# Sixteen small matmul tiles for the key features of three batches, with new transposes, products and schedule

## The chip, the cores and the metric

The kernel runs on one core of a Trainium2 chip. The metric is the device time of one execution in microseconds (us); smaller is better. Every kernel was run several times, in rounds together with runs of the kernel before on the same chip; experiments 10 to 12 and 13 ran on other chips than 1 to 9, so across them compare ratios and not medians. A run counts as "slow" when it is over 1.5% above the fastest of the same kernel, and "fast" otherwise; on a single core the two words say no more than that. A ratio is the mean time of one kernel's fast runs over that of the other's fast runs of the same rounds, so it is not quite the ratio of the medians quoted beside it.

One more number is used throughout: the **MLP span**, from the start of the first hidden-layer matmul to the start of the last output matmul, both read from TensorE's timeline. Before it lies the head (attention of batch 0), behind it a tail of 3.5 us that is the same in all kernels here.

## The reference, cut to what matters

```python
def phi(x):                                   # r = 8, so 64 features for a row of 32
    a = einsum('rd,bhsd->bhsr', S1, x)
    b = einsum('rd,bhsd->bhsr', S2, x)
    return einsum('bhsi,bhsj->bhsij', a, b).reshape(..., r * r)
q_p, k_p = phi(q), phi(k)                     # q, k, v: 4 batches, 4 heads, 1088 rows, 32 columns
kv  = einsum('bhsf,bhsd->bhfd', k_p, v)
z   = sum(k_p, axis=2)
num = einsum('bhsf,bhfd->bhsd', q_p, kv)
den = einsum('bhsf,bhf->bhs', q_p, z)[..., None] + 1e-06
x = (num / den) transposed to 4352 x 128
h = x @ w_in                                  # 128 x 2048
g = maximum(h, 0) + alpha * minimum(h, 0)
out = g @ w_out                               # 2048 x 128
```

## The kernel before

The program makes its own schedule: each operation is declared with the engines that may do it, an assumed duration in ns, its buffers and a wished time, and a planner orders all of them and gives out the buffers. So the engines execute fixed orders that were tuned for assumed durations. Seven PSUM banks are shared by attention and MLP.

For batches 1 to 3 the old code makes the key features in two halves per batch. VectorE turns 32x32 blocks of k, TensorE multiplies with a block-diagonal S1, S2 (`S12blk`), the result (a and b side by side) is copied from PSUM, and GpSimd forms the 64 products of each row.

```python
def turn(dst, hp=hp):                                     # VectorE, two per half
    nc.vector.transpose(dst...[:, x], k_sb[b][:, 2 * hp:2 * hp + 2]...[:, x])
def fe(e):                                                # TensorE, 16 matmuls per half, 128x32 tiles
    for j in range(n):
        for i in range(0, cnt, aw):
            nc.tensor.matmul(ps(bf)[lo + i:lo + i + aw, j * 64:(j + 1) * 64], sb(bT)[:, ...], S12blk..., start=True, stop=True)
# (copy to ab on ScalarE or VectorE cut)
def pr(e, i=i):                                           # GpSimd: one instruction per half, 16 rows x 64 products
    i0 = bview(at_(a, i * m * r), [[r, m], [1, r], [0, r]])
    i1 = bview(at_(a, r * n * H + i * m * r), [[r, m], [0, r], [1, r]])
    nc.gpsimd.tensor_tensor(out=dst, in0=i0, in1=i1, op=ALU.mult)
res.append(op(en, {"dve": dv(64 * m), "pool": 110 + 64 * m * 1.8}, pr, ...))
```

The products then go into the `kv` matmuls, which sum over all rows and need every product of the batch. The z part is one Gram matmul per group of rows (`zs`), four small ones for the batch's 64 last rows (`zr`), a mask on VectorE (`zm`) and one folding matmul (`finz`):

```python
def zr(e):
    for h in range(H):
        nc.tensor.matmul(ps(bzs)[32 * h:32 * h + r, z0:z0 + r], ab_rest[m][rest, 0, h], ab_rest[m][rest, 1, h], ...)
o = op("pe", 270, lambda e: nc.tensor.matmul(ps(bf)[:, 128:256], E8..., zt(), start=True, stop=True), ..., name=f"finz{b}")
```

Dummy matmuls on constants keep TensorE busy in the head: seven of 512 columns as a warm-up, and a few that the planner puts into idle stretches.

```python
def dummy(n=1):
    for _ in range(n):
        nc.tensor.matmul(PS[:, 7], ones(128), ones(512), start=True, stop=True, skip_group_check=True)
op("pe", 3750, lambda e: dummy(7), due=-1e6, name="warm", ni=14)
o.fill = max(0, int((t - free_at["pe"] - 150) / DUMMY)) if 4000 < t < FILL and not begun else 0
```

## Time and profile before

| | kernel before |
|---|---|
| median of its runs beside the changed kernel | 113.86 us (113.24 to 114.72, 4 runs) |
| span of the profiled run | 112.2 us |
| first MLP matmul, MLP span | 16.98 us, 91.77 us |
| GpSimd busy | 24.2 us (22%) |

The prediction below shows the lines that carry the main reading. Four more are needed to read what came of the change. First the GpSimd products among the groups by form (line, engine, operation, tiles, shapes, count; then busy us and mean ns; then the idle time before them and what ended it):

```profile
L652 POOL TENSOR_TENSOR kp__71<-ab__68 128x1024 f32<-128x1024 f32 x3 | 5.9, 1954 | 17.7 <-ACT ab__68 L360 17.7
```

Two such instructions make a batch, 3.9 us. Then one stretch of the sums by stretch (columns as in the prediction), in the middle of the MLP; GpSimd has a single instruction there:

```profile
47.00:60.00 13.00, 12.79 (x196) 6.41 (x197) 8.44 (x17) 9.94 (x20) 1.95 (x1) 1.00 0.13 23
```

Then the folding matmul, as its source line is listed (fastest, median and slowest record in ns; eight records are two fp32 passes for each of four batches):

```profile
L756 PE MATMUL ps<-fs__99,E x8: 271/275/377, 10.6 to 80.3; 128*128 128x128 f32 x8
```

Last, the weight loads of TensorE just after a half of key features:

```profile
65.91 0.11 PEld L974 LDWEIGHTS <-w_a_bf 128*128 128x128 bf16 x2
```

Two output-weight loads start at 65.91 us, yet the first matmul recorded after them starts at 66.14. One matmul has no record. This line was not consulted for the prediction, and it should have been.

### The profile page before, as it was taken

How to read it: one execution, taken by the hardware profiler on the slowest of the kernel's cores; microseconds unless marked ns; L12 is line 12 of the kernel's file. 1: busy time of each engine (PE TensorE's matmuls, PEld its weight loads, DVE VectorE, ACT ScalarE, POOL GpSimd, SP SyncE). 2: the span in 40 equal slices, each digit the busy share in tenths (PEclk: the TensorE clock that was granted, in tenths of full speed). 3: DMA queues.
4: the chain of work that ended last, by engine and by line, in shares of the span. 5: the costliest groups of instructions: out<-in, count | busy, mean ns of one | idle time of the engine just before them, and what ended most of it. 6: DMA issues, size and time to landing. Idle time of an engine off the chain costs nothing.

```text
span 112.2 us, 3530 instructions
## 1 busy us (share of the span) xinstructions
PE 104.2 (93%) x1444; PEld 53.6 (48%) x1459; DVE 81.7 (73%) x155; ACT 76.4 (68%) x166; POOL 24.2 (22%) x24
## 2 busy tenths in 40 slices
PE   7997789989999999999999999999999999999980
PEld 2475223634446433465543243454543354588870
DVE  3186869799994869985657997574988987377850
ACT  2454489996369765776876665983754688697860
POOL 3052089992042027300600015000000000000000
PEclk9999999999999999999999999999999999999999
DMA  2998899859849951023003200410050023042231
GB/s 64 268 280 237 256 273 341 179 119 353 149 85 363 183 86 30 0 49 50 6 0 57 37 6 0 69 24 6 0 93 0 0 44 56 0 73 41 35 53 47
DMA packets 37536, 11.25 MB, mean 100 GB/s; under 512 B 27008, under 2 KB 37520, under 8 KB 37520
## 3 DMA queue, kind: packets, MB, share of 16 engines
q1 hardware_dynamic: 37264, 10.95, 41.4%
q8 instruction: 11, 0.18, 0.8%
q10 hardware_dynamic: 256, 0.08, 0.3%
q14 instruction: 5, 0.04, 0.1%
HBM read 8.80 MB, written 2.23 MB: 98 GB/s over the span
## 4 chain that ended last, share of the span: by engine, by line
PE 55%; SPq 12%; DVE 11%; DMA 11%; issue 4%; ACT 3%; DVEq 0%
PE ps L974 21%; PE ps L953 18%; SPq L384 10%; DMA k<-in_k_dram 7%; PE ps L784 6%; PE ps L827 4%; DMA out_dram<-oT__91 3%; PE ps L635 3%; DVE kT__64 L680 1%; DMA out_dram<-oT__92 1%; DVE winT L362 1%; SPq L1001 1%; DVE qT__74 L814 1%; PE ps L705 1%; DVE kT__66 L680 1%
## 5 line engine op out<-in xcount | busy, mean ns | idle before, releaser
L953 PEld LDWEIGHTS <-w_in_bf 128*128 128x128 bf16 x160 | 14.8, 98 | 17.0 <-issue 5.6
L953 PE MATMUL ps<-xT__96,w_in_bf 128*128 128x512 bf16 (+1 forms) x77 | 21.3, 357 | 0.9 <-DVE winT L362 0.3
L974 PEld LDWEIGHTS <-w_a_bf 128*128 128x128 bf16 x144 | 13.7, 98 | 13.8 <-issue 2.0
L953 PE MATMUL ps<-xT__97,w_in_bf 128*128 128x512 bf16 (+1 forms) x78 | 19.0, 336 | 0.3 <-issue 0.2
L959 ACT ACTIVATE rh__82<-ps 128x512 bf16<-128x512 f32 (+1 forms) x19 | 10.6, 560 | 6.7 <-PE ps L732 2.4
L959 ACT ACTIVATE rh__83<-ps 128x512 bf16<-128x512 f32 (+1 forms) x18 | 10.0, 554 | 3.1 <-PE ps L953 2.5
L652 POOL TENSOR_TENSOR kp__70<-ab__67 128x1024 f32<-128x1024 f32 (+1 forms) x4 | 6.9, 1731 | 20.7 <-ACT ab__67 L360 13.8
L652 POOL TENSOR_TENSOR kp__71<-ab__68 128x1024 f32<-128x1024 f32 (+1 forms) x4 | 6.9, 1733 | 17.7 <-ACT ab__68 L360 17.7
L959 ACT ACTIVATE rh__84<-ps 128x512 bf16<-128x512 f32 (+1 forms) x17 | 9.4, 551 | 1.2 <-PE ps L953 0.7
L959 ACT ACTIVATE rh__85<-ps 128x512 bf16<-128x512 f32 (+1 forms) x15 | 8.4, 558 | 1.1 <-PE ps L974 0.5
L959 ACT ACTIVATE rh__87<-ps 128x512 bf16<-128x512 f32 (+1 forms) x15 | 8.1, 539 | 1.0 <-PE ps L953 0.8
L959 ACT ACTIVATE rh__86<-ps 128x512 bf16<-128x512 f32 (+1 forms) x13 | 7.3, 564 | 2.1 <-PE ps L784 2.1
L360 ACT COPY aq__76<-ps 128x1024 f32<-128x1024 f32 (+2 forms) x8 | 5.7, 757 | 4.0 <-PE ps L827 3.3
L959 ACT ACTIVATE rh__88<-ps 128x512 bf16<-128x512 f32 (+1 forms) x11 | 5.9, 537 | 2.9 <-PE ps L953 1.9
L981 DVE STREAM_TRANSPOSE oT__91<-ps 128x512 f32<-128x512 f32 (+1 forms) x8 | 5.4, 679 | 3.1 <-PE ps L974 3.0
L841 DVE TENSOR_TENSOR aq__76<-ps,aq__76 128x1024 f32<-128x1024 f32 (+1 forms) x6 | 5.6, 952 | 2.3 <-PE ps L827 2.3
L974 PE MATMUL ps<-rh__83,w_a_bf 128*128 128x512 bf16 (+1 forms) x19 | 6.8, 357 | 0.3 <-issue 0.3
L791 DVE STREAM_TRANSPOSE dt__78<-ps 128x1024 f32<-128x1024 f32 (+2 forms) x6 | 5.6, 930 | 1.8 <-PE ps L784 1.6
L827 PE MATMUL ps<-qT__74,Sab 32*64 32x512 f32 x96 | 6.7, 613 | 0.0
L974 PE MATMUL ps<-rh__82,w_a_bf 128*128 128x512 bf16 (+1 forms) x18 | 6.5, 361 | 0.1
L974 PE MATMUL ps<-rh__86,w_a_bf 128*128 128x512 bf16 (+1 forms) x18 | 6.4, 355 | 0.2 <-issue 0.2
L974 PE MATMUL ps<-rh__85,w_a_bf 128*128 128x512 bf16 (+1 forms) x18 | 6.4, 356 | 0.1
(149 smaller groups left out, 209.7 us busy)
## 6 DMA issues: line engine op xcount, KB each, us to landing
out_dram<-oT__91 SPq DMA_DIRECT2D x28, 64.0 KB, 1.9
k<-in_k_dram SPq DMA_DIRECT2D x3, 512.0 KB, 4.1
q<-in_q_dram SPq DMA_DIRECT2D x3, 512.0 KB
v<-in_v_dram SPq DMA_DIRECT2D x12, 128.0 KB, 5.7
w_in_f<-in_moe_w_in_dram SPq DMA_DIRECT2D x2, 512.0 KB, 7.9
w_out_f<-in_moe_w_out_dram SPq DMA_DIRECT2D x2, 512.0 KB, 7.3
k<-in_k_dram SPq DMA_DIRECT2D x2, 256.0 KB, 3.3
q<-in_q_dram SPq DMA_DIRECT2D x2, 256.0 KB, 3.5
```

The lines of the kernel that those rows point to most:

```text
L360: nc.scalar.copy(dst, src)
L384: (nc.sync if eng == "sp" else nc.scalar).dma_start(dst, src)
L635: nc.tensor.matmul(ps(bf)[lo + i:lo + i + aw, j * 64:(j + 1) * 64], sb(bT)[:, j * cnt + i:j * cnt + i + aw], S12blk.rearrange("p h c -> p ...
L652: (nc.vector if e == "dve" else nc.gpsimd).tensor_tensor(out=dst, in0=i0, in1=i1, op=ALU.mult)
L784: nc.tensor.matmul(dst, w, mv, start=True, stop=True, skip_group_check=True)
L791: nc.vector.transpose(bview(sb(dt), [[1, nn]]).rearrange("p (c n) -> p c n", c=2), ps(bd)[:, :, :ncp])
L827: nc.tensor.matmul(ps(bufs[t // 2])[64 * c:64 * c + 64, t % 2, :nf], bview(Sab[32 * t:32 * t + 32, i], [[1, R]]), moving(sb(bq), t, c), st ...
L841: nc.vector.tensor_mul(a, told(ps(b2[x])[:, :, :nf]), a)
L953: nc.tensor.matmul(ps(b)[:, :n], w_in_bf[:, c * 128:(c + 1) * 128], xs(), start=True, stop=True)
L959: nc.scalar.activation(sb(br)[:, :n], ps(b)[:, :n], ACTF.Relu)
L974: nc.tensor.matmul(ps(bo)[:, :n], w, y(), start=c == 0, stop=c == NC)
L981: o = op("dve", dv(n) + 40, lambda e: nc.vector.transpose(bview(sb(boT), [[1, n]]), ps(bo)[:, :n]), [last], [bo, boT], 80, end, f"oT{g}")
```

## The change

The intent is to take TensorE time out of the key features. S1 and S2 become a 32x16 weight; the whole turned batch streams through sixteen 32x32 tiles at once, which gives a and b with the feature on the partition axis. VectorE then turns them back in 32x32 blocks straight from PSUM, and GpSimd multiplies what it finds there, with an operand whose innermost step is four floats. The z term of the last rows gets its own columns and its own folding matmul with 32 rows. In the head, the first queries are copied in quarters, the reciprocal's scratch leaves the denominator's bank (so the dummies shrink from 512 to 480 columns), and a new rule cuts dummies that would push needed work over what the planner takes for an instruction-block boundary (`BLOCK`, 256 instructions). Most of the several hundred tuned planner offsets are new.

```diff
+        if not pe:
+            bT, bp = Buf("qT"), [pq(), pq()]
+            def turn(e):                         # two transposes of 512 for the batch
+                ...
+            def fe(e):
+                for g in range(4):
+                    for c in range(4):
+                        nc.tensor.matmul(ps(bp[g // 2])[32 * c:32 * c + 32, g % 2, :256], bview(S12[32 * g:32 * g + 32], [[1, 32]]),
+                                         bview(sb(bT)[32 * g:32 * g + 32], ...)[:, :, 32 * c:32 * c + 32], start=True, stop=True)
+            o = op("pe", 600, fe, [o, c_S12], [bT] + bp, 200, due + 2, f"k{b}ab", mode=2, ni=64)
+            for x in range(2):
+                def back(e, x=x, bab=bab):
+                    for g in range(2):
+                        nc.vector.transpose(bview(part(sb(bab), 2 * g), [[128, H], [1, 2], [4, 32]]),
+                                            ps(bp[x])[:, g, :256].rearrange("p (h j f) -> p h j f", h=H, j=2))
+                a = op("dve", 1050, back, [o], [bp[x], bab], 80, due + 3, f"k{b}.{x}abT")
+                for y in range(2):
+                    def pr(e, bab=bab, bkp=bkp, y=y):
+                        for h in (2 * y, 2 * y + 1):
+                            i0, i1 = [part(sb(bab), 128 * h + 32 * z) for z in range(2)]
+                            nc.gpsimd.tensor_tensor(out=..., in0=bview(i0, [[1, 4], [4, r], [0, r]]),
+                                                    in1=bview(i1, [[1, 4], [0, r], [4, r]]), op=ALU.mult)
+                    ks.append(op("pool", 220 + 512 * 1.8, pr, [a], [bab, bkp], 80, due + 4, f"k{b}.{x}kp{y}"))
 # ... z term of the last rows, batches 1 to 3:
+                nc.tensor.matmul(ps(bzs)[:32, z0 + 32:z0 + 64], f[0], f[1], start=False, stop=True, skip_group_check=True)
+            nc.tensor.matmul(ps(bf)[:, 128:256], (F8 if b else E8)..., zt(), start=True, stop=not b)
+            if b:
+                nc.tensor.matmul(bview(ps(bf)[:, 128:256], [[32, H], [1, r]]), E8[:32]..., z_rest[b], start=False, stop=True)
 # ... head:
+            while o.fill and t < there.get((count + 2 * o.fill + o.ni) // BLOCK, 1e9) + 500 > there.get((count + o.ni) // BLOCK, 1e9) + 500:
+                o.fill -= 1
-            nc.tensor.matmul(PS[:, 7], ones(128), ones(512), start=True, stop=True, skip_group_check=True)
+            nc.tensor.matmul(PS[:, 7, :480], ones(128), ones(480), start=True, stop=True, skip_group_check=True)
-            t = ps(bd)[:, 0, :nb] if first else sb(dt)[:, :nb, 0]
+            t = PS[:, 7, 480:480 + nb] if first else sb(dt)[:, :nb, 0]
-            for x in range(2):
-                ac.append(op(("act", "dve"), ad(512), ...))       # query copies per half
+            for x in range(4):
+                ac.append(op(("act", "dve"), ad(256), ...))       # per quarter
 # ... planner offsets, masks, buffer classes cut
```

## The prediction

> **What bounds the kernel now.** I read the page's busy shares first, then the busy sums by stretch, the chain of waits, TensorE's own waits, and last the timelines of TensorE, VectorE and ScalarE. The page says which engine is full and that its clock is never cut:
>
> ```profile
> PE 104.2 (93%) x1444; PEld 53.6 (48%) x1459; DVE 81.7 (73%) x155; ACT 76.4 (68%) x166; POOL 24.2 (22%) x24
> PEclk9999999999999999999999999999999999999999
> ```
>
> The sums by stretch (columns: stretch, its length, then busy us of each engine) show that this holds from about 17 us on, and where a second engine is full too:
>
> ```profile
> 17.00:22.00 5.00, 4.93 (x71) 2.59 (x75) 4.38 (x8) 5.00 (x13) 5.00 (x6) 1.00 0.95 269
> 22.00:30.00 8.00, 7.61 (x92) 3.39 (x85) 7.86 (x16) 5.65 (x10) 3.75 (x3) 1.00 0.91 220
> 30.00:38.00 8.00, 7.70 (x162) 4.06 (x157) 6.37 (x11) 5.94 (x13) 1.95 (x1) 1.00 0.85 208
> 38.00:47.00 9.00, 8.79 (x133) 3.68 (x134) 7.33 (x15) 5.92 (x13) 3.91 (x2) 1.00 0.33 52
> ```
>
> From 17 us to about 108 us TensorE is the bound: it carries the MLP and, between its matmuls, the attention work of batches 1 to 3. Its longest waits in the whole span are under a microsecond each, and those over 0.3 us lie before about 24 us. So a microsecond of TensorE work taken out is worth nearly one of the time, provided VectorE, which is full from 22 to 30 us, does not give it back. Before 17 us a dependence chain through batch 0 sets the start of the MLP; a gain there shifts everything behind it. Its end in TensorE's timeline:
>
> ```profile
> 13.19 0.82 PE L498 MATMUL ps<-const-bfloat16-1.0 128*128 128x512 bf16 x3 [0.16 <-issue]
> 14.49 1.04 PE L498 MATMUL ps<-const-bfloat16-1.0 128*128 128x512 bf16 x4 [0.48 <-issue]
> 15.47 0.66 PE L784 MATMUL ps<-aq__76,kvW 64*32 64x256 f32 x16
> 16.06 0.69 PE L871 MATMUL ps<-qT__74,Sab 32*64 32x256 f32 x16
> 16.98 1.28 PE L953 MATMUL ps<-xT__96,w_in_bf 128*128 128x512 bf16 x5 [0.24 <-DVE xT__96 L806]
> ```
>
> Seven dummy matmuls (L498) sit ahead of the numerator (L784 with kvW), and the second lot begins after 0.48 us without a wait that the profile can name. VectorE has the other operand early:
>
> ```profile
> 14.18 0.26 DVE L798 RECIPROCAL dt__78<-ps 128x16 f32<-128x16 f32 x1
> 14.48 0.71 DVE L800 STREAM_TRANSPOSE rr__80<-dt__78 128x512 f32<-128x512 f32 x1
> 16.24 0.69 DVE L806 TENSOR_TENSOR xT__96<-ps,rr__80 128x512 bf16<-128x512 f32 x1 [1.05 <-PE ps L784]
> ```
>
> The reciprocals are turned at 15.19, but the product waits 1.05 us for the numerator.
>
> [...] in the 128x32 key features, passes start four at a time, 7 ns apart, every 56 ns; in the 32x64 query features all eight first passes start within 50 ns. No record of before uses 16. [...] The new products read with a step of four floats, 16 bytes. The old ones do not, so the trace of before cannot test it; it only gives the base, 1.95 us for 1024 elements.
>
> **The change part by part.**
>
> TensorE, key features. Now each of batches 1 to 3 has two halves of 16 fp32 matmuls, 32 records, six halves in all:
>
> ```profile
> 65.40 0.58 PE ps L635 x32
> 65.98 0.16 issue
> 66.14 1.24 PE ps L974 x5
> ```
>
> These lines are from the chain of waits. The half's own passes take 0.58 us, but what it displaces is more: from the preceding MLP matmul, which starts at 65.02, to the next at 66.14 are 1.12 us, of which one MLP matmul takes 0.216 us. So 0.91 us is lost, entry and exit included. The other five stand beside other attention work, and by the same subtraction cost 0.55 to 0.95 each. Six come to an estimated 4.9 us. After: three stages of 16 matmuls of 32x32 with 256 moving columns. The 32x64 query stage of 512 columns (L827) displaces 1.14 us between two MLP matmuls; its passes are 0.43 us apart for 512 columns and 0.216 us for 256 (L871), so one with 256 displaces about 1.14 - 2 x 0.213 = 0.71 us. Eight more tiles at 7 ns add 0.05: 0.77 us, and three come to 2.3 us if sixteen tiles run at once as eight do. Saved: 4.9 - 2.3 = 2.6 us.
>
> TensorE, the rest. The z term of the 64 last rows goes from four small matmuls to one for a batch; eight records at about 17 ns become two, -0.1 us each. The folding of z gets a second matmul, two fp32 passes of 32 columns, an estimated +0.12 us each against the 0.25 us that the one now displaces. Together about zero. The kv products stay as they are. Net on TensorE: 2.5 us less.
>
> VectorE. Each batch gains four transposes of 128x256 from PSUM. A 128x512 from PSUM takes 0.72 us, a 128x256 0.45 us (the oT rows); the strided 128x256 of keys 0.60 to 0.70 us. Taking 0.55: +2.2 us a batch, +6.6 in all. The four strided key transposes of a batch (2.2 us) become two of 512 elements, estimated at 0.9 to 1.0 us each: -0.3 us a batch. With the extra masks (early, in a 2.4 us idle stretch) VectorE goes from 82 to about 88 us. ScalarE loses six feature copies at 0.37 us, one of them VectorE's already: about -2 us. The two together rise from 158 to some 162 us out of 224, so the load fits, if relu work moves to ScalarE.
>
> GpSimd. The products keep 2048 elements a batch but become eight instructions with a step of 16 bytes: [...] it is on no path that I find, since batch 1's products have from about 25 to 33 us.
>
> The head. The reciprocal's scratch goes out of the denominator's PSUM bank into the last columns of bank 7, so the numerator gets its bank when the denominator has been turned (13.93) and not after the reciprocal (14.44). The new fill rule stops dummies from being pushed over an instruction-block boundary just ahead of needed work. If the numerator is done by 15.2, x follows the turned reciprocals at about 15.25 and not at 16.24: 1.0 us. The first query's copies in quarters start after a part of its matmuls, but cost four more instructions on ScalarE and VectorE; I count them as +-0.2. The first weight chunk is cast by 13.7 and the first scaled output weights by 15.6, so they allow a start at 16.0. I count 0.9 us.
>
> Sum: 2.5 + 0.9 = 3.4 us if nothing comes back. I take 0.4 us off for stalls by the four-bank hold, three times, and for VectorE between 20 and 47 us: 3.0 us. 113.85 - 3.0 = 110.85, say 110.9 us (-2.6%).
>
> **Rivals.** First, VectorE becomes the bound from 20 to 47 us. For: it works 21.6 of the 25 us from 22 to 47, and two batches' extra transposes add some 4 us, which alone would fill it. Against: ScalarE has 7.5 us idle there and takes relus, and the whole schedule is retuned. It would give back 1 to 2 us: 112 to 113 us. Second, PSUM: the feature stage holds four of the seven shared banks until VectorE has read them, and the MLP's hidden banks run short. For: after query stages, which hold as many, idle times of 0.2 us occur. Against: only three such stages. Worth 0.3 to 1 us: 111.2 to 112. Third, the head gain is hidden, because ScalarE is full from 17 to 22 us casting weights and DMA moves 269 GB/s then: an earlier first matmul would only wait later. That costs 0.9 us: 111.8. Fourth, the sixteen tiles do not run together[...]: a stage of 1.2 us leaves 1.2 of the 2.5 us saved, 112.1.
>
> **Range and chances.** All of the gain without loss is 110.4, and a retuned schedule that also shrinks the small gaps early on could reach 109.5; two rivals together give 112.8. The three runs of before spread 1.3%. So 109.3 to 112.8 for 8 in 10. The line of 2% is at 111.57, 0.7 above my value: faster 0.60, same 0.37, slower 0.03, since nothing that I find adds TensorE work.
>
> **What would show it.** Right: three feature groups of 32 records with 256 columns, each displacing 0.7 to 0.85 us; the first MLP matmul near 16.0 us; the kv and MLP groups as long as now; VectorE 86 to 89 us busy, ScalarE about 74[...], and TensorE still at 93% of a shorter span. Wrong: TensorE's waits grow to microseconds with VectorE or ScalarE as releaser between 20 and 47 us (first rival), waits for PSUM right after a feature stage (second), an early first matmul with longer gaps before 24 us (third), or a feature stage over 1.1 us (fourth).

## The result, and the profile after

| | before | after |
|---|---|---|
| median | 113.86 us (113.24 to 114.72, 4 runs) | 118.21 us (117.62 to 118.96, 4 runs) |
| ratio of fast runs | | 1.038, 95% interval 1.0287 to 1.0473 |
| span of the profiled run | 112.2 us | 115.6 us |
| first MLP matmul | 16.98 us | 17.41 us |
| MLP span | 91.77 us | 94.66 us |

The changed kernel is slower by 3.8%, and the prediction of 110.9 us was wrong. Of the 3.3 us between the two profiled spans (112.22 and 115.56), 2.9 lie in the MLP span and 0.4 in the head. Busy times of the whole page, and its chain of waits; above them the chain by engine of the kernel before:

```profile
PE 55%; SPq 12%; DVE 11%; DMA 11%; issue 4%; ACT 3%; DVEq 0%
```

```profile
PE 107.7 (93%) x1354; PEld 53.8 (47%) x1354; DVE 87.6 (76%) x168; ACT 75.4 (65%) x164; POOL 32.9 (28%) x44
...
PE 71%; POOL 9%; ACT 8%; DVE 3%; DMA 3%; issue 1%; POOLq 1%; SPq 1%; ACTq 0%
PE ps L1014 22%; PE ps L1035 20%; PE ps L845 7%; POOL kp__68 L723 5%; POOL kp__69 L723 5%; PE ps L888 3%; DMA kr<-in_k_dram 3%; PE ps L753 3%; ACT rh__81 L1020 2%; PE ps L932 2%; PE ps L502 2%; PE ps L1032 2%; ACT aq__75 L363 2%; PE ps L613 2%; ACT w_hl L363 1%
```

The loads of VectorE and ScalarE are close to what was predicted (about 88 and 74 us). GpSimd's went from 24.2 to 32.9 us, and it stands on the chain with 9% now, through the products (L723); before it had no place on it. TensorE's own waits say the same (in total us, times, longest):

```profile
PE ps L753 <- POOL kp__68 L723: 0.9, 2, 0.5
PE ps L1035 <- ACT rh__81 L1020: 0.9, 1, 0.9
...
PE ps L1014 <- ACT rh__81 L1020: 0.7, 1, 0.7
```

**The kv matmuls wait for GpSimd.** The stretch that answers to the one shown of before, in which GpSimd went from one instruction to eight:

```profile
47.00:60.00 13.00, 12.55 (x197) 5.28 (x196) 10.53 (x16) 8.20 (x16) 6.08 (x8) 1.00 0.13 23
```

GpSimd's timeline in it, and TensorE's at its end:

```profile
50.48 1.56 POOL L723 TENSOR_TENSOR kp__68<-at__101 128x256 f32<-128x256 f32 x2 [17.46 <-PE ps L1014]
51.99 3.06 POOL L723 TENSOR_TENSOR kp__69<-at__100 128x256 f32<-128x256 f32 x4
54.99 1.57 POOL L723 TENSOR_TENSOR kp__68<-at__101 128x256 f32<-128x256 f32 x2
```

```profile
55.61 0.54 PE L753 MATMUL ps<-kp__68,v 128*32 128x64 f32 x6
56.61 0.58 PE L753 MATMUL ps<-kp__68,v 128*32 128x64 f32 x25 [0.45 <-POOL kp__68 L723]
```

Eight products run back to back for 6.1 us. TensorE starts the kv matmuls of batch 2 when most products are there, and stops in the middle until the last ones are. Only 0.45 us is booked as a wait; from the first kv pass at 55.61 to the next MLP matmul at 57.86, with the Gram matmuls behind it, the group takes 2.2 us, against 1.3 us in experiment 5, where nothing is waited for. The same happens in batch 3 at about 80 us (2.5 us against 1.4). Together the two groups are some 2.0 us longer. TensorE is "busy" at 93% in both kernels, and that number hid it: of the 0.9 us by which this group is longer, half is booked as a wait (0.45 us) and the rest as work.

The fixed order has a share in it that no run here isolates. In batch 2 GpSimd begins with `at__101`, the half that VectorE turned last (ready at 50.31 us, `at__100` at 49.39), and it makes the second pair of `kp__68` last of all, although TensorE reads `kp__68` first.

**The folding is dearer.** In TensorE's timeline:

```profile
60.86 0.38 PE L814 MATMUL ps<-fs__98,F 128*128 128x128 f32 x2
61.17 0.40 PE L816 MATMUL ps<-zr,E 32*128 32x32 f32 x2
61.51 0.39 PE L1035 MATMUL ps<-rh__84,w_a_bf 128*128 128x512 bf16 x1
```

From 60.86 to the next MLP matmul at 61.51 are 0.65 us. The first matmul alone displaced 0.25 us before, so the second one, with a quarter of the rows and of the columns, costs 0.40 us: its 32-row tile starts 0.31 us after the one before it and the MLP 0.34 us after that.

**The head gained nothing.** TensorE's timeline up to the first output matmul:

```profile
13.23 0.63 PE L845 MATMUL ps<-aq__75,kvW 64*32 64x256 f32 x15
14.34 0.40 PE L845 MATMUL ps<-aq__75,kvW 64*32 64x256 f32 x1 [0.48 <-issue]
14.83 1.60 PE L502 MATMUL ps<-const-bfloat16-1.0 128*128 128x480 bf16 x7
16.36 1.12 PE L932 MATMUL ps<-qT__72,Sab 32*64 32x256 f32 x32
17.41 0.82 PE L1014 MATMUL ps<-xT__95,w_in_bf 128*128 128x512 bf16 x3
19.08 0.38 PE L1035 MATMUL ps<-rh__81,w_a_bf 128*128 128x512 bf16 x1 [0.85 <-ACT rh__81 L1020]
```

The numerator starts at 13.23 instead of 15.47, as the prediction had it, and x is ready at 16.35 us (VectorE's product starts at 15.66 and takes 0.69) instead of 16.93. But seven dummies hold the second query group until 16.36, and that group, now whole (32 records) where half of it used to start at 11.75, holds the first MLP matmul until 17.41. Then the first output matmul waits 0.85 us for its relu, and ScalarE's timeline shows why:

```profile
17.61 0.92 ACT L363 COPY aq__75<-ps 128x256 f32<-128x256 f32 x3 [1.74 <-PE ps L932]
18.41 0.63 ACT L1020 ACTIVATE rh__81<-ps 128x512 bf16<-128x512 f32 x1
```

The relu comes behind three of the quarter copies in ScalarE's fixed order, and those wait for the query group that ran at 16.36.

**The sixteen tiles did what was wanted.** By start-to-start subtraction the three stages displaced 0.74, 0.74 and 0.87 us of MLP work, where 0.77 was predicted. In the stage at 22.66 us all sixteen first passes start within 0.10 us.

### The profile page after: what moved, and what is told of

Read it like the earlier page. It is cut to its first block, busy times and chain, and to the rows that moved or that the text cites. A ratio compares the mean times of both kernels' runs of the same rounds, so it can differ in the third digit from the quotient of the medians.

```text
span 115.6 us, 3384 instructions
## 1 busy us (share of the span) xinstructions
PE 107.7 (93%) x1354; PEld 53.8 (47%) x1354; DVE 87.6 (76%) x168; ACT 75.4 (65%) x164; POOL 32.9 (28%) x44
## 4 chain that ended last, share of the span: by engine, by line
PE 71%; POOL 9%; ACT 8%; DVE 3%; DMA 3%; issue 1%; POOLq 1%; SPq 1%; ACTq 0%
PE ps L1014 22%; PE ps L1035 20%; PE ps L845 7%; POOL kp__68 L723 5%; POOL kp__69 L723 5%; PE ps L888 3%; DMA kr<-in_k_dram 3%; PE ps L753 3%; ACT rh__81 L1020 2%; PE ps L932 2%; PE ps L502 2%; PE ps L1032 2%; ACT aq__75 L363 2%; PE ps L613 2%; ACT w_hl L363 1%
## 5 line engine op out<-in xcount | busy, mean ns | idle before, releaser
L1014 PE MATMUL ps<-xT__95,w_in_bf 128*128 128x512 bf16 (+1 forms) x80 | 22.1, 359 | 0.8 <-ACT rh__81 L1020 0.7
L1014 PE MATMUL ps<-xT__96,w_in_bf 128*128 128x512 bf16 (+1 forms) x80 | 20.3, 337 | 0.0
L1020 ACT ACTIVATE rh__81<-ps 128x512 bf16<-128x512 f32 (+1 forms) x23 | 13.0, 565 | 3.4 <-PE ps L1014 2.1
L1020 ACT ACTIVATE rh__83<-ps 128x512 bf16<-128x512 f32 (+1 forms) x17 | 9.9, 581 | 4.9 <-PE ps L1014 4.9
L1020 ACT ACTIVATE rh__82<-ps 128x512 bf16<-128x512 f32 (+1 forms) x19 | 10.3, 543 | 3.6 <-PE ps L1014 3.5
L723 POOL TENSOR_TENSOR kp__68<-at__101 128x256 f32<-128x256 f32 x8 | 6.3, 810 | 17.5 <-PE ps L1014 17.5
L1020 ACT ACTIVATE rh__84<-ps 128x512 bf16<-128x512 f32 (+1 forms) x16 | 8.9, 554 | 2.5 <-PE ps L1014 2.5
L1035 PE MATMUL ps<-rh__81,w_a_bf 128*128 128x512 bf16 (+1 forms) x25 | 9.1, 363 | 0.9 <-ACT rh__81 L1020 0.9
L363 ACT COPY aq__75<-ps 128x256 f32<-128x256 f32 (+1 forms) x11 | 6.2, 617 | 5.2 <-PE ps L888 2.8
L723 POOL TENSOR_TENSOR kp__68<-at__100 128x256 f32<-128x256 f32 x4 | 3.1, 799 | 19.1 <-PE ps L1035 19.1
L1035 PE MATMUL ps<-rh__82,w_a_bf 128*128 128x512 bf16 (+1 forms) x23 | 8.3, 361 | 0.0
L1020 ACT ACTIVATE rh__85<-ps 128x512 bf16<-128x512 f32 (+1 forms) x14 | 7.3, 525 | 1.4 <-PE ps L1014 1.3
L1035 PE MATMUL ps<-rh__83,w_a_bf 128*128 128x512 bf16 (+1 forms) x22 | 7.9, 361 | 0.0
L1020 ACT ACTIVATE rh__86<-ps 128x512 bf16<-128x512 f32 (+1 forms) x13 | 7.1, 550 | 0.3 <-PE ps L1035 0.3
L1035 PE MATMUL ps<-rh__84,w_a_bf 128*128 128x512 bf16 (+1 forms) x20 | 7.1, 353 | 0.0
L902 DVE TENSOR_TENSOR aq__75<-ps,aq__75 128x1024 f32<-128x1024 f32 x4 | 4.8, 1205 | 2.6 <-PE ps L888 2.6
L502 PE MATMUL ps<-const-bfloat16-1.0 128*128 128x480 bf16 x18 | 5.7, 458 | 0.9 <-PEq L1111 0.8
L1035 PE MATMUL ps<-rh__85,w_a_bf 128*128 128x512 bf16 (+1 forms) x18 | 6.4, 356 | 0.0
```

Source lines behind the costliest of these rows:

```text
L363: nc.scalar.copy(dst, src)
L502: nc.tensor.matmul(PS[:, 7, :480], ones(128), ones(480), start=True, stop=True, skip_group_check=True)
L723: nc.gpsimd.tensor_tensor(out=bview(part(sb(bkp), 256 * h), [[R, 4], [r, r], [1, r]]), in0=bview(i0, [[1, 4], [4, r], [0, r]]), in1=bview( ...
L902: nc.vector.tensor_mul(a, told(ps(b2[x])[:, :, :nf]), a)
L1014: nc.tensor.matmul(ps(b)[:, :n], w_in_bf[:, c * 128:(c + 1) * 128], xs(), start=True, stop=True)
L1020: nc.scalar.activation(sb(br)[:, :n], ps(b)[:, :n], ACTF.Relu)
```

## The experiments

The starting theory: the loss is in what has to read the tiles' result, first the strided products on GpSimd (about 2 us), then the second folding matmul (1 us), then the order of the head (1 us). The rivals: the kv matmuls are merely placed too early in the order; VectorE or PSUM banks are the limit; or something outside the change's text, such as the chip's clock, sets the time. Unless said otherwise the order of all engines is that of the changed kernel, only the named edit differs, and the result is correct.

**1. The kv matmuls later in the order.**

```diff
-    for o in plan(ops, classes):
+    planned = plan(ops, classes)
+    later = {'kv2': 3200, 'kv3': 2475, 'kvr3': 1250, 'zm3': 600}      # ns
+    for o in planned:
+        o.start += later.get(o.name, 0)
+    for o in sorted(planned, key=lambda o: o.start):
```

> The changed kernel with the key-value products of batches 2 and 3 placed later in TensorE's order: batch 2's behind seven MLP matmuls more, batch 3's behind five more (1.1 us). Nothing else moves. Theory of the blocked queue: in the changed kernel TensorE reaches these products before GpSimd has finished the features (groups of 2.2 us where batch 0 and 1 need about 1.3), and being in order it stands still; moved, the two groups fall to about 1.2-1.3 us each and the time falls by 1.6 to 1.9 us, from 118.2 to about 116.4. Rival, the schedule hides nothing and the wait only moves (MLP buffers or the product chain become the limit): time within 0.5 us of 118.2.

Measured: 119.87 us (119.26 to 121.06, 4 runs), ratio 1.0573 (1.0482 to 1.0665), 1.9% slower than the change itself by the two ratios. Neither the theory's 116.4 us nor the rival's 0.5 us around 118.2 came. The stalls inside the kv groups are gone, but a new wait stands first among TensorE's:

```profile
PE ps L1014 <- DVE aq__75 L902: 1.3, 3, 0.6
```

The MLP matmuls that now stand where kv stood find their PSUM banks still held by query products that VectorE has not read. What follows: these shifts only move the wait, as there was no MLP work with a free bank to put in its place. The products have to be done earlier, or faster.

**2. The second folding matmul with all 128 rows**, 96 of them zero.

```diff
-    z_rest = [consts.tile([32, 32], F32, ...)]
+    z_rest = [consts.tile([128, 32], F32, ...)]                  # zeroed once
-                nc.tensor.matmul(..., E8[:32].rearrange(...), z_rest[b], start=False, stop=True)
+                nc.tensor.matmul(..., E8.rearrange(...), z_rest[b], start=False, stop=True)
```

> The changed kernel with the second folding matmul of z run over all 128 rows (the rest's z lies in a tile padded with zeros) and not over 32 rows; result unchanged, order unchanged. [...] with full rows it adds about 0.12 and the folding displaces 0.35-0.4, three times -0.27: time -0.8 us, to 117.4. Rival, the cost is that of two dependent fp32 matmuls as such: the displacement stays at 0.6 or more, time within 0.3 us of 118.2.

Measured: 118.21 us (117.57 to 119.52, 4 runs), ratio 1.0414 (1.035 to 1.0478). In TensorE's timeline of batch 2:

```profile
63.09 0.39 PE L816 MATMUL ps<-fs__98,F 128*128 128x128 f32 x2
63.31 0.31 PE L818 MATMUL ps<-zr,E 128*128 128x32 f32 x2
63.46 0.38 PE L1037 MATMUL ps<-rh__84,w_a_bf 128*128 128x512 bf16 x1
```

Both foldings now displace 0.37 us instead of 0.65, in all three batches, so four times the rows cost 0.28 us less. The second matmul starts 0.22 us after the first and the MLP 0.15 us after that; with the tile of 32 rows it was 0.31 and 0.34. So the cost came with the tile of 32 rows, at its entry and at its exit, and not with the amount of work. Three times 0.28 would be 0.85 us; the MLP span fell by 0.48 us to 94.18, and the median did not move. Runs that spread by 2 us cannot show so small a gain, so the expected 0.8 us of time is not shown. The spread became a question of its own (below).

**3. The products with unit step** (wrong values on purpose: the operands are read at the wrong places).

```diff
-  in0=bview(i0, [[1, 4], [4, r], [0, r]]), in1=bview(i1, [[1, 4], [0, r], [4, r]])
+  in0=bview(i0, [[r, 4], [1, r], [0, r]]), in1=bview(i1, [[r, 4], [0, r], [1, r]])
```

> The changed kernel, order unchanged, with GpSimd's feature products reading their 32 numbers with a step of one float in place of four (a wrong result on purpose, the same count of elements). Theory of the strided read: one product of 256 elements falls from 0.80 us to about 0.55, eight from 6.1 to about 4.3 us, so TensorE's two stalls in front of the key-value products (0.95 us each) vanish: time -1.7 to -2 us, about 116.3. Rival, the 0.8 us are the fixed cost of eight short instructions in place of two: the products stay at 0.75 or more and the time within 0.4 us of 118.2.

Measured: 115.59 us (115.4 to 117.65, 4 runs), ratio 1.0196 (1.0147 to 1.0246). The products in the groups by form, first of the changed kernel, then of this one:

```profile
L723 POOL TENSOR_TENSOR kp__68<-at__101 128x256 f32<-128x256 f32 x8 | 6.3, 810 | 17.5 <-PE ps L1014 17.5
```

```profile
L723 POOL TENSOR_TENSOR kp__68<-at__101 128x256 f32<-128x256 f32 x8 | 4.8, 627 | 18.7 <-PE ps L1014 18.7
```

One product falls from 0.81 to 0.63 us, the eight of such a group from 6.3 to 4.8 us busy. That is +29% for an instruction with the step of 16 bytes. The old products took 1.07 us for 512 and 1.95 us for 1024 elements, so the fixed part of an instruction is an estimated 0.19 us; without it the step adds an estimated (0.81 - 0.19) / (0.63 - 0.19), about 40%. The step is the only edit, and the kv stalls of 2.0 us vanish, the MLP span falls by 2.06 us to 92.60 and the ratio by 1.8% (some 2.1 us). This is the largest single part of the loss, and it belongs to an engine that is idle 72% of the time.

**4. Without the seven dummies ahead of the second query group.**

```diff
+    for o in planned:
+        o.fill = {'q0.1a': 0}.get(o.name, o.fill)
```

> The changed kernel without the seven dummy matmuls that stand ahead of the second query half (14.8 to 16.4 us). Theory of the fill: these dummies delay that half, then the MLP's first matmul (17.41) and the relus behind ScalarE's four query copies; without them the half starts at about 14.9, the first MLP matmul follows its x at 16.4 and the 0.85 us wait for the first relu shrinks: time -1.0 to -1.8 us, 116.4 to 117.2. Rival, the start is set elsewhere (weights' casts, instruction fetch): first MLP matmul within 0.3 us of 17.4, time within 0.4 us of 118.2[...].

Measured: 117.87 us (116.23, 117.04, 118.70, 118.72), ratio 1.0294 (1.0215 to 1.0373). The first output matmul's wait for its relu falls from 0.85 us to

```profile
PE ps L1035 <- ACT rh__81 L1020: 0.3, 1, 0.3
```

and the MLP span by 0.56 us to 94.10. The shorter wait comes from the missing dummies and not from this run's late start: experiment 5, which starts as late with the dummies, waits 0.9 us, and experiment 13, early and without them, 0.3. The ratio's interval overlaps with that of the change and rests on two fast runs, so a gain in time is not shown. Its profiled run, a slow one, began the MLP at 19.07 us, 1.7 us later than the changed kernel's. The reason is in a different place, see 6.

**5. A layout in which products read with unit step and are right.** The back transposes write runs of eight floats, the last rows' z goes back into the main block as before the change, and the second folding matmul disappears.

```diff
-  nc.vector.transpose(bview(part(sb(bab), 2 * g), [[128, H], [1, 2], [4, 32]]), ...)
+  nc.vector.transpose(bview(part(sb(bab), 16 * g), [[128, H], [r, 2], [32, 4], [1, r]]), ...)
-  in0=bview(i0, [[1, 4], [4, r], [0, r]]), in1=bview(i1, [[1, 4], [0, r], [4, r]])
+  in0=bview(i0, [[r, 4], [1, r], [0, r]]), in1=bview(i1, [[r, 4], [0, r], [1, r]])
-  # zr, zm, finz: separate block, second mask, second matmul for b > 0
+  # zr, zm, finz as in the kernel before
```

> The changed kernel with the turned features laid out token group by token group (each a and b block of 8 features in consecutive floats): GpSimd then reads with a step of one float, the z of the last rows lands in the same PSUM block as before the change, and the second folding matmul is gone. Same order of all engines, result unchanged. Theory of the two added costs: products at 0.63 us as in the unit-stride run, the key-value groups of batches 2 and 3 without stalls (1.2-1.3 us), the z folding back at 0.25-0.35 us; first to last MLP matmul 94.7 - 2.1 - 1.0 = 91.6 us, as before the change (91.8); median about 115.0. Rival, the write in runs of 8 floats makes VectorE's turning slower than 0.53 us a piece, or further stalls step in: first to last MLP matmul over 92.8 us.

Measured: 116.84 us (114.83 to 118.16, 6 runs), ratio 1.0159 (1.01 to 1.0218; two of six runs are fast ones, the others fall under the 1.5% rule). Products 0.63 us, folding 0.22 to 0.26 us, MLP span 92.23, no kv stalls. A gain that had not been looked for: the back transposes themselves, whose line in the list of sources is

```profile
L715 DVE STREAM_TRANSPOSE at__100<-ps x6: 406/408/450, 25.9 to 74.8; 128x256 f32<-128x256 f32 x6
```

408 ns instead of 615 ns in the changed kernel, for the same elements written in runs of eight floats instead of singly with a step of 16 bytes. It repairs what experiments 2 and 3 found together, with a correct result. The MLP span is near the theory's 91.6 us and under the rival's 92.8; the median missed the theory's 115.0, and the profiled run is a slow one.

**6. Why runs of one kernel spread by 2 us.** In some profiled runs the same early matmuls take nearly twice as long. First the kernel of experiment 2, then the changed kernel (TensorE's timelines):

```profile
7.34 1.12 PE L654 MATMUL ps<-S12blk,kT__64 128*64 128x64 f32 x16
8.40 2.01 PE L934 MATMUL ps<-qT__72,Sab 32*64 32x256 f32 x32
```

```profile
6.51 0.69 PE L652 MATMUL ps<-S12blk,kT__64 128*64 128x64 f32 x16
7.12 1.12 PE L932 MATMUL ps<-qT__72,Sab 32*64 32x256 f32 x32
```

TensorE is slower at the start: in the changed kernel's profiled run seven dummies of 480 columns take 2.96 us from 0.78 us on, and 1.60 us from 14.83. The page's row of tenths shows full speed throughout, so one has to see it in durations, or in the trace's own record of the clock, whose full-speed stretch begins at 5.3 us in the changed kernel's profiled run and at 12.3 us in that of experiment 2. The full-speed stretches of all 14 profiled runs are 102.40, 105.81, 109.23 or 112.64 us long, in steps of 3.41 us, and their starts differ. Why one starts late is not shown. All profiled runs, by number of the experiment (6 is no run):

| kernel | full clock from | first MLP matmul | MLP span |
|---|---|---|---|
| before | 3.8 us | 16.98 | 91.77 |
| after | 5.3 | 17.41 | 94.66 |
| 1 kv later | 4.6 | 17.94 | 95.93 |
| 2 full rows | 12.3 | 19.73 | 94.18 |
| 3 unit step | 4.4 | 17.40 | 92.60 |
| 4 no dummies | 12.6 | 19.07 | 94.10 |
| 5 new layout | 9.6 | 19.15 | 92.23 |
| 7 512 columns | 3.9 | 17.52 | 94.72 |
| 8 transpose earlier | 4.3 | 18.60 | 94.75 |
| 9 all four | 12.5 | 19.04 | 91.33 |
| 10 ten dummies | 4.2 | 17.99 | 94.71 |
| 11 casts later | 3.7 | 16.52 | 92.16 |
| 12 fills and casts | 3.6 | 16.75 | 91.96 |
| 13 fills | 4.0 | 16.71 | 91.15 |

Where the clock came at 9.6 us or later, the MLP began at 19.0 to 19.7 us; where it came by 5.3 us, at 16.5 to 18.6 us. The four late ones (2, 4, 5, 9) are also the four profiled runs that count as slow; the ten early ones are all fast. No other run has its clock on record. A late start as such does not shorten the MLP span much: 7, 8 and 10 begin at 17.5 to 18.6 us and have 94.71 to 94.75.

A late clock is not all that goes with a late start. VectorE turns the first queries when their DMA has landed; first the changed kernel, then experiment 8:

```profile
6.25 0.71 DVE L915 STREAM_TRANSPOSE qT__72<-q 128x512 f32<-128x512 f32 x1 [0.34 <-DMA q<-in_q_dram]
7.55 0.71 DVE L915 STREAM_TRANSPOSE qT__72<-q 128x512 f32<-128x512 f32 x1 [2.03 <-DMA q<-in_q_dram]
```

In the six early starts with the changed kernel's head (after, 1, 3, 7, 8, 10) the first MLP matmul follows this transpose by 11.0 to 11.3 us, and the transpose starts anywhere from 6.21 to 7.55 us. So the late 18.60 us of experiment 8, with its clock at 4.3 us, goes with late queries.

**7. The warm-up with 512 columns as before the change.**

```diff
-    op("pe", 3750, lambda e: dummy(7), due=-1e6, name="warm", ni=14)
+    op("pe", 3750, lambda e: dummy(7, 512), due=-1e6, name="warm", ni=14)
```

> The changed kernel with the seven warm-up matmuls at 512 columns as before the change and not 480. Theory of the clock: TensorE's full clock starts in the records at 3.8 us before the change and at 4.4 to 12.6 us in the profiles after it, [...] the full clock starts at 3.8 to 5.5 us in the profile and the spread of the times shrinks under 1 us, median 117.3 to 117.8. Rival, the wait for the last rows' keys (placed ahead of the second half's keys by the new order) is what breaks the warm-up: the late start at 12 us and the spread of 1.3 us or more stay.

Measured: 118.87 us (117.64 to 119.41, 6 runs), ratio 1.0464 (1.041 to 1.0518). The spread stays at 1.8 us: the shorter dummies are not what makes it, at least not alone.

**8. The second key transpose ahead of that of the last rows**, as in the kernel before.

```diff
+    later = {'kr0.0T': 180}
```

> The changed kernel with one transpose moved: that of the last rows' keys behind that of the second half's keys, as before the change; the warm-up stays at 480 columns. Theory that the wait for the last rows' keys (0.2 to 0.9 us at 5 us) lets the clock's start slip: full clock from under 6 us in the profile, spread of the times under 1 us, median 117.3 to 117.8. Rival, the shorter warm-up alone decides: the late start and a spread of 1.3 us or more stay, as in the changed kernel.

Measured: 118.56 us (117.7 to 120.22, 6 runs), ratio 1.0418 (1.0373 to 1.0463). No gain and no smaller spread. By itself this order is not the cause either. The profiled run has the early clock that the theory asked for, and yet a late start, by its queries (6).

**9. All four repairs**: the layout of 5, the warm-up of 7, the order of 8, and no dummies as in 4.

> All four edits at once on the changed kernel: token-group layout, 512-column warm-up, second half's keys first, and no dummies ahead of the second query half. Theory that these are the costs that the change brought besides its gain: 118.2 - 3.1 (layout) - 1.2 (dummies) - 0.5 (clock) = 113.4 us, about equal to before (113.2 to 113.9), spread under 1 us. Rival, another cost of the new schedule stays (ScalarE and VectorE full from 22 to 38 us): 114.5 us or more, with waits of TensorE for ScalarE or VectorE of over 1.5 us between 17 and 30 us.

Measured: 114.17 us (113.31 to 116.46, 22 runs), ratio 1.0044 (1.002 to 1.0067). The MLP span is 91.33 us, for the first time below before's 91.77. The times fall into two groups: 15 runs up to 114.75 and 7 from 115.18 to 116.46 us; before had 2 of 27 above 115.1 in the same rounds. The median lies between the theory's 113.4 us and the rival's 114.5; the expected spread of under 1 us did not come.

**10. Ten warm-up dummies of 512 columns** in the changed kernel, nothing else.

```diff
+    op("pe", 3750, lambda e: dummy(10, 512), due=-1e6, name="warm", ni=14)
```

> The changed kernel with a warm-up of ten dummy matmuls of 512 columns in place of seven of 480 (TensorE busy with bfloat16 rows from 0.8 to about 5.1 us at the slow clock, so the first key transposes start 0.6 to 1.2 us later). Theory (part of the loss and its spread of 117.6 to 119.5 us is a late start of TensorE's full clock, which [...]comes at 3.8 to 5.3 us in one start and at 9.6 to 12.6 us in another): the full clock is on by 6 us in every start, no time above 119.0, spread under 1.5 us, median 117.6 to 118.3 (what the early starts lose by the later head, the late ones gain). Rival (the spread is something else): spread as before, over 2 us, and the median 0.5 to 1 us longer than the changed kernel's 118.2, near 119.

Measured: 118.56 us (118.08 to 118.67, 6 runs), ratio 1.0401 (1.0355 to 1.0447). The spread is 0.6 us, as against 1.3 to 2.5 us for the change and experiments 2, 7 and 8, and no run is above 119.0. This fits the clock as a cause of the spread; with six runs, one of them profiled, it does not show it, and the late queries of 6 would spread the times too. The median came out 0.26 us above the expected upper end, and no better than the change's. Whether the longer warm-up costs in every run what the late starts lose is not shown: this run's MLP start of 17.99 us goes with queries that were turned at 6.94. But the clock is not the loss: the changed kernel's fastest run, the profiled one with an early clock, is still 3.6 us above the profiled run of before (117.62 and 114.0).

**11 and 12. Two casts on ScalarE behind a relu, without and with early dummies.** In experiment 9 the MLP waits 0.72 us at 26.6 us for a relu that stands behind two casts of output weights. Experiment 11 moves the relu ahead of them; 12 adds three dummies in the gaps of the first key transposes (and in 12 and 13 the planner's other dummies have 512 columns again).

```diff
+    later = {'kr0.0T': 180, 'w_hi0': 890, 'w_hi3': 540, 'r0.10': -188}
 # 12 only:
+        o.fill = {'q0.1a': 0, 'k0.1T': 2, 'kr0.0ab': 1}.get(o.name, o.fill)
```

> The kernel with all four repairs, and two casts of the output weights on ScalarE moved behind one relu instead of ahead of it. Theory (ScalarE's order holds TensorE for 0.72 us at 26.6 us, and this is on the path): TensorE's wait at 26.6 goes or falls under 0.2 us, the MLP span falls from 91.3 to about 90.7 us, and the fast cluster from 113.3-114.7 to 112.8-114.1; two clusters stay. Rival (VectorE is full there and the winT copies follow at once, so the next wait takes its place): MLP span within 0.2 us of 91.3.

> The same with three dummy matmuls in the gaps of the first key transposes (two ahead of the second transpose, one ahead of the first features of the last rows). Theory (late starts of the clock make the upper cluster): times of the upper cluster, 8 of 22 over 115.1 us with all four repairs, become at most 2 of 22, the full clock is on by 7 us in the profile, and the median is 113.0 to 113.6, equal to before's or below it. Rival (the two clusters are not the clock's start): as many in the upper cluster, the median 0.3 us up.

Measured: 114.43 us (114.01 to 116.88, 22 runs), ratio 1.0058 (1.0033 to 1.0084) for 11; 114.55 us (113.75 to 116.25, 22 runs), ratio 1.0056 (1.0028 to 1.0084) for 12. Moving the casts did not help: the ratios are within each other's intervals, and the profiled MLP span of 11 is 92.16 us, 0.8 us longer than in 9. In 11 the wait that replaced the old one is

```profile
PE ps L1001 <- ACT winT L363: 1.0, 1, 1.0
```

because the copies of the transposed input weights, right behind the casts, hold a PSUM bank that the MLP needs. The rival was right about the next wait, though the span grew where it expected none of over 0.2 us. The dummies cut the runs over 115.1 us from 9 of 22 in 11 to 4 of 22 in 12, less than the expected 2, and the median is not the expected 113.0 to 113.6 (and the 8 of 22 that the expectation counts for experiment 9 are 7).

**13. The four repairs and the early dummies, casts as they were.**

> The kernel with all four repairs and the three early dummy matmuls, with the casts and the relu in their old order. Theory (the dummies bring the clock on early in most starts; the moved casts were what cost the other two kernels time, by holding the bank that the winT copies read): at most 3 of 22 times over 115.2 us where the four repairs alone have 7 of 22, the times under 115 at 113.3 to 114.4, median 113.7 to 114.0, which is before's within 0.5%. Rival (the dummies themselves cost the 0.4 us, by delaying the second key transposes): median 114.4 to 114.6 as with the casts moved.

Measured: 114.04 us (113.14 to 115.42, 22 runs), ratio 1.0031 (1.0003 to 1.006). One of 22 runs is above 115.1 us where experiment 9 had 7, and the mean of all runs goes from 114.60 to 114.01 (before's, in the rounds of each: 113.74 and 113.82). That more early dummies leave fewer slow runs is shown by 9 and 13, and by 11 and 12; that they do it through the clock is not: the profiled run of 13 has the full clock from 4.0 us and that of 9 from 12.5, but 11 and 12 have it from 3.7 and 3.6. The same matmuls as in 6, now at full speed from about 4 us:

```profile
6.82 0.69 PE L652 MATMUL ps<-S12blk,kT__64 128*64 128x64 f32 x16
7.44 1.12 PE L919 MATMUL ps<-qT__72,Sab 32*64 32x256 f32 x32
```

The median is just above the upper end of what the theory expected, and well below the rival's 114.4. This version is some 4 us faster than the changed kernel, and 0.3% behind the kernel before. No version here beats the kernel before.

## Why the prediction was wrong, point by point

- **GpSimd: "it is on no path that I find".** This is the step that failed. The products take 6.1 us a batch, and took 3.9 before. What the step would cost was the author's estimate, which the trace of before could not test; experiment 3 parts the two causes: eight short products with unit step take 4.7 us (batch 2), and the step adds 29% to an instruction. And no date was compared with the cost: in their order batch 2's products start when both halves are turned back (50.5 us) and the kv matmuls stand at 55.6 us in TensorE's order, before the last products are done at 56.6. Experiment 3 measures the step of 16 bytes alone: 2.06 us of MLP span, 1.8% of the time. The diff carried a warning: the planner assumed 220 + 512 x 1.8 = 1142 ns for a pair of products, and a pair took 1.6 us (1.17 us with unit step), so the retuned order is tuned for products that the chip does not run. "The whole schedule is retuned" was used as an argument against the rivals, and it was one for them.
- **"an estimated +0.12 us each" for the second folding matmul.** It cost 0.40 us, three times; rows and columns were counted, and the change of tile shape was not. Experiment 2 shows that: with full rows both matmuls displace 0.37 us. The -0.1 us for the last rows' z did not appear: with the kv part they stand beside, 0.38 us both before and after.
- **"So 0.91 us is lost, entry and exit included".** The interval of 1.12 us holds two MLP matmuls and not one; the first has no record, as the weight loads at 65.91 us show. With two, the half cost 0.69 us. Six of those would be 4.1 us, less the 2.35 us measured for the three new stages, so the saving is an estimated 1.8 us and not 2.6. The 0.16 us "issue" piece in the chain that was quoted as part of the half was that missing matmul.
- **"the first MLP matmul near 16.0 us".** Numerator and x came early, as worked out, and then the seven dummies and the whole second query group stood ahead of the MLP: 17.41. The new fill rule was read as removing dummies ahead of needed work, and seven remained. The first relu then came late through ScalarE's fixed order (0.85 us, experiment 4: 0.3 us).
- **"its clock is never cut".** The row PEclk shows that, but the same run's record of the clock has full speed only from 3.8 us on (experiment 6). No term of the sum hung on it.
- **VectorE as the bound (first rival)** did not happen as a bound. It appears as one cause of late banks, in experiment 1. The second rival, held banks, is what made that experiment fail. The third, a head gain hidden by ScalarE, had no head gain to hide; experiment 13 speaks against it, as its MLP starts 2.3 us earlier than in experiment 9 and its span is no longer (91.15 and 91.33). The fourth, the tiles not running together, was refuted.
- **"slower 0.03, since nothing that I find adds TensorE work".** Work was the wrong measure. The change took a chain of TensorE, copy, GpSimd and made it TensorE, VectorE, GpSimd with slower parts behind, and with the schedule's order frozen a late producer costs TensorE time directly.

What stays open: with all repairs the MLP span is only 0.4 to 0.6 us shorter than before's, against the estimated 1.8 us saved. The waits for relus behind casts near 26 us (0.7 us) are a candidate, as those copies were partly VectorE's work before; a repair that holds was not found, so that is argued, not shown. Nor was the order retuned for the real durations, which the kernel's authors could do. And the 21 fast runs of experiment 13 still spread over 1.7 us (113.14 to 114.80); the arrival of the first queries (6) is a candidate that no run isolates.

## What to carry to other kernels

When a result leaves one engine in a new layout, price the readers in that layout first, and compare the date at which the last reader is done with the date at which the bound engine needs it; an engine that is 72% idle can still be late. A schedule tuned for assumed durations is worth as much as those durations, so read them in the diff and hold them against the trace. And before a displacement is taken between two matmuls, count the weight loads between them.
